# Attention with squared ReLU, then a feed-forward layer: one more batch in block form, and loads in permuted order

## The chip, the cores and the metric

The kernel runs on one core of one Trainium2 chip. The metric is the device time of one execution in microseconds. An execution is described by a profile with the times of every instruction on TensorE (PE, with its weight loads PEld), VectorE (DVE), ScalarE (ACT), GpSimd (POOL) and the queue of SyncE (SP), and of the DMA transfers.

## The reference, cut to what matters

There are 8 batches of 12 heads with 448 positions and 64 numbers a head. The attention has no softmax: scores are rectified, squared and divided by the length. Its output, 3584 rows of 768, goes through a layer to 2048 columns, an exact GELU, and a layer back to 768.

```python
scores = scale * np.matmul(q, k.transpose(0, 1, 3, 2))
attn = np.maximum(scores, 0.0) ** 2 / S
attn_out = np.matmul(attn, v)
x = attn_out.transpose(0, 2, 1, 3).reshape(B * S, H * D)
h = x @ w_in
g = 0.5 * h * (1.0 + erf(h * inv_sqrt2))
return g @ w_out
```

## The kernel before, in words

Inputs come as float32 and are cast to bf16 by the loading DMAs, which GpSimd issues. A batch is worked in three groups of four heads (g = 0 to 2), and each group in seven blocks of 64 key rows (i = 0 to 6).

**Attention.** One score step (`fn_qk`, L686) makes four 64x64 tiled matmuls of 448 columns into a PSUM pair. ScalarE (L698) or VectorE (L700) rectifies and scales it into a bf16 tile `a_sq`, and VectorE squares that in place (L707). After seven steps, `add_av` (L746) multiplies by the values, 28 matmuls, and two copies bring the result to `xT` (L400 and L402 are the lines of the copy helper).

**Feed-forward.** `add_f1` makes one tile of the first layer, 128 of the 2048 columns: six matmuls of 448 columns (L800) and a GELU on ScalarE (L810) into the ring `h_sb`, which holds two batches. The second layer goes over 14 groups of 256 rows (`add_group`, L1108); each group is a two-by-two block product done with seven products instead of eight, at the price of sums on VectorE (L1089, L1142). The first 256 rows are done plainly (L1203).

**Block form of the first layer.** For batches 5, 6 and 7 (`add_blocks`, L942) the first layer also takes seven products instead of eight, on halves of the inner dimension, of the columns and of the 448 rows, so that a matmul has 224 columns. It needs sums of weight quarters (`add_wsums`, L867), made once while batch 7's attention runs, sums of the input's quarters (L909), and adds of partial results (L976).

**Order of the work.** A planner written in Python runs when the program is built. It knows a duration for each operation, due times worked out over several passes, and how many buffers there are, and fixes each engine's order. The first part of the order is written out by hand (`ORDER`: a letter for the engine, a number for the operation). From batch 2 on, TensorE's order is a fixed list. Batches 0 and 1 do their attention beside the first layer of batch 0. Batches 2 to 7 each have six slots, and after each slot come as many feed-forward products as a share (`SHARES`) gives it:

```python
            x = [("QK", (b, g, i, None)) for i in range(NK)]
            mid = ("AV", done) if done else ("FFN", None)
            out.append(x[:2] + [mid] + x[2:4])
            out.append(x[4:])
```

So a group's value product stands among the first steps of the next group. The products that fill the slots are the rest of batch 1's first layer, the plain rows, groups 1 to 6, and the first layers of batches 2, 3 and 4. After the last value product come, with no attention beside them, the blocks of batches 5 to 7 woven with groups 7, 9 and 11, and the groups 8, 10, 12 and 13.

**Queries and keys.** A score step needs both transposed. Batches 0 and 1 are loaded contiguously and transposed by TensorE. Batch 2 is loaded contiguously too, and VectorE copies it in permuted order (`permute_k` L529, `permute_q` L540) into the pair `pq`, `pk`. From batch 3 on, `add_wide` loads queries and keys in that permuted order straight into the pair, 64 numbers to a run: six DMAs of keys (L467) and twelve of queries (L476) for a batch. The one pair serves all batches, so a load waits until the transposes of the batch before have read it (`war`). From the pair, SP issues seven transposing DMAs (`add_T_dma`, three for keys at L632, four for queries at L641) into `kT` and `qT`, which exist twice. They're allowed from a given slot of the batch before on.

**GpSimd's queue** is strictly in order. It holds the loads of batches 0, 1 and 2 and the first layer's weights, the first part of the second layer's weights `wout` (L372), a small copy `gate` that waits for the transposed queries of batch 2 (L653), the other two parts of `wout`, batch 3's keys, queries and values, and then for each batch a gate and the load of the batch after next.

Of the kernel before, what the change touches and what calls it, by code (L numbers as in the profile page):

```python
# [13 lines left out]
KC = 112  # L14
# [21 lines left out]
T_TWO = 0.72  # L36
# [8 lines left out]
DMA_FREE = 4.54  # L45
# [8 lines left out]
SHARES = (1.3, 1.0, 1.0, 1.0, 1.0, 1.0)  # L54
LAST = 256
PASSES = 5
NEAR = 0.5
# [4 lines left out]
WIDE = 2.0  # L62
# [13 lines left out]
G0 G1 G2 G3 G4 G5 A10 D13 G6 A16 P11 P14 G7 D12 A15 P17 G8 D18 P21 P39 D22 P33 P36 A34 D40  # L76
P19 D20 A37 P23 G9 P42 P48 D24 P54 A43 D35 A49 P51 D44 P25 D38 A52 D41 G117 A55 D53 P45 D50
A26 D47 A46 P57 D56 P69 P66 A58 D70 P27 G118 A67 P29 D59 P63 G119 A28 D71 P60 A64 G120 D68
P78 D61 A62 P75 A79 D65 P81 P31 D30 A76 D80 P96 G121 D32 A97 P72 D77 G122 A82 D98 P129 G123
D74 A73 P90 D130 P84 P108 A91 G124 D83 P131 A85 D109 P93 P141 D132 A94 D92 P102 D95 P105  # L80
P111 A103 D86 P143 D110 G125 A106 D104 P99 A112 D107 G126 A144 P87 D100 A101 D113 A142 P157
P114 D88 G127 A158 D89 P133 D115 A116 G128 P135 D159 A134 P160 P163 D136 P166 A164 P145 D167
A161 D165 P253 A146 D168 D162 P169 P172 G147 A254 P175 A173 D170 P245 G148 A176 D171 P255
A246 D177 G149 D174 P184 P187 A256 P196 A185 G150 D188 P137 P139 A138 P178 D197 G151 A140
D186 P193 P211 G152 D180 P247 A212 G153 D213 P249 A248 D179 A194 D198 G154 P263 A250 D195
D229 G155 P223 P220 A264 D189 P190 S235 A224 D221 P265 G156 A191 D225 P267 A266 D192 D222
P199 P217 A268 P214 D231 A218 P257 S236 D215 A200 D219 P259 A258 D216 D201 P181 P208 A260
P205 D230 A209 P261 D182 P251 D183 A262 D210 A206 D233 P202 A252 S237 D207 D232 P226 D234
A203 D204 S238 S239 P269
# [17 lines left out]
class Scheduler:  # L107
# [151 lines left out]

    def place(self, fixed):  # L260
# [14 lines left out]
        while rest or any(fixed.values()):  # L275
# [7 lines left out]
            for e, v in fixed.items():  # L283
                if v and not (e == "PE" and by.get("PE")):
                    tops.append(self.pick(v[:1]))
# [11 lines left out]
def kernel(  # L297
# [37 lines left out]
    def get_nat(b):  # L335
        if b not in nq:

            tq, tk = ("pq", "pk") if b == 1 else ("nq", "nk")
            nq[b] = natpool.tile([KC, H, NC * D], BF16, tag=tq, name="nq")
            nk[b] = natpool.tile([128, HP, NK * D], BF16, tag=tk, name="nk")  # L340
            vt[b] = vpool.tile([128, HP, NK * D], BF16, tag="v", name="v_sb")

# [34 lines left out]
    pqk = []  # L377

    def get_p():
        if not pqk:  # L380
            pqk.append(natpool.tile([KC, NC, DM], BF16, tag="pq", name="pq"))
            pqk.append(natpool.tile([128, G, NK * 128], BF16, tag="pk", name="pk"))
        return pqk
# [40 lines left out]
    def war(b):  # L424

        old = [o for (bb, *_), o in list(Pq.items()) + list(Pk.items()) if bb == b - 1]
        c = {1: -1, 2: 0}.get(b, b - 1)
        old += [o[0] for (bb, *_), o in list(Tq.items()) + list(Tk.items()) if bb == c]
        return old
# [19 lines left out]
    def add_v(b, g0, g1):  # L449
        def fn():  # L450
            get_nat(b)
            nc.gpsimd.dma_start(vt[b][:, 2 * g0 : 2 * g1], kv_view(v, b, g0, g1))  # L452

        old = [o for (bb, *_), o in AV.items() if bb == b - 3]
        o = dma(fn, (g1 - g0) * 4 * S * 256, old)
        for g in range(g0, g1):
            ld_v[b, g] = [o]

    def add_wide(b):


        def k_fn(e):
            def fn():
                to = get_p()[1].rearrange("p g (i e d) -> e p g i d", e=2, d=D)
                src = kv_view(k, b, 0, G).rearrange("p (g e) (i d) -> e p g i d", e=2, d=D)
                for g in range(G):
                    nc.gpsimd.dma_start(to[e][:, g], src[e][:, g])  # L467

            return fn

        def q_fn(e, j):
            def fn():
                to = get_p()[0].rearrange("p c (g j e d) -> j e g p c d", j=2, e=2, d=D)
                src = q[b].rearrange("(g e j) (p c) d -> j e g p c d", e=2, j=2, c=NC)
                for g in range(G):
                    nc.gpsimd.dma_start(to[j][e][g], src[j][e][g])  # L476

            return fn

        def v_fn():  # L480
            vt[b] = vpool.tile([128, HP, NK * D], BF16, tag="v", name="v_sb")
            nc.gpsimd.dma_start(vt[b], kv_view(v, b, 0, G))

        n = G * 4 * S * 256
        ks = [dma(k_fn(e), WIDE * n / 2, war(b), G) for e in range(2)]
        qs = [dma(q_fn(e, j), WIDE * n / 4, war(b), G) for e in range(2) for j in range(2)]
        old = [o for (bb, *_), o in AV.items() if bb == b - 3]
        o = dma(v_fn, n, old)
        ops = Both(ks), Both(qs)
        for g in range(G):  # L490
            ld_v[b, g] = [o]
            Pk[b, g] = ops[0]
            for c in range(NC):
                Pq[b, g, c] = ops[1]

    class Both:


        def __init__(self, ops):
            self.ops = ops  # L500

        @property
        def done(self):
            ends = [o.done for o in self.ops]
            return None if None in ends else max(ends)

    def add_load(b, g0=0, g1=G):
        if b > 2:
            return add_wide(b)
        add_k(b, g0, g1)  # L510
        add_q(b, g0, g1)
# [14 lines left out]

    def permute_k(copy, g, src):

        copy(  # L529
            get_p()[1][:, g].rearrange("p (i e d) -> p e i d", e=2, d=D),  # L530
            src.rearrange("p e (i d) -> p e i d", d=D),
        )

    def permute_q(copy, g, c0, c1, src):

        dst = get_p()[0][:, c0:c1, 256 * g : 256 * g + 256].rearrange(
            "p c (j e d) -> e p j c d", j=2, d=D
        )
        for e in range(2):
            copy(dst[e], src[:, 2 * e : 2 * e + 2].rearrange("p j (c d) -> p j c d", d=D))  # L540

    def add_pk(b, g0, g1, after=(), bias=0.0):
        for g in range(g0, g1):
            deps = ld_k[b, g] + list(after)
            deps += [Tk[max(b - 1, 1), x, i][0] for x in range(G) for i in range(NK)]
            Pk[b, g] = sch.add(
                (("DVE", 0.31, 0.43),),
                lambda e, g=g: permute_k(V.tensor_copy, g, nk[b][:, 2 * g : 2 * g + 2]), deps,
                bias=bias,
            )  # L550

    def add_pq(b, g0, g1, c0=0, c1=NC, after=(), bias=0.0):
        for g in range(g0, g1):
            deps = [ld_q[b, g, c] for c in range(c0, c1)] + list(after)
            deps += [Tq[max(b - 1, 1), g, c][0] for c in range(c0, c1)]
            if b == 2:
                deps += [Tq[1, x, c][0] for x in range(G) for c in range(NC)]
# [896 lines left out]
```

## Time and profile before

| What | Value |
|---|---|
| time, median of three runs | 371.25 us (370.54 to 372.1) |
| the profiled execution | 370.77 us |
| its span, first to last instruction | 368.9 us |
| TensorE busy | 358.9 us, 97% of the span |
| VectorE busy | 288.3 us, 78% |
| ScalarE busy | 200.8 us, 54% |
| GpSimd busy | 108.0 us, 29% |
| software DMA queue | 74,992 packets, 22.47 MB, 58.6% of 16 engines |
| hardware DMA queues (SP's) | 38,768 packets, 19.46 MB, 26.8% |
| TensorE's granted clock | 0.999 |

Busy shares are means over stages. From about 65 to 252 us the attention of batches 2 to 7 runs with its feed-forward products between; from 252 to 364 the closing products alone. Times of single matmuls in the profile overlap, as they're pipelined, so a group's length is read from where the next one starts. A wait is put down to the one that came last.

### The profile page before, as it was taken

Reading aid. Unit: us, or ns where it says so; the run is one execution under the profiler, and the core shown is the slowest. Engines: PE = TensorE matmul, PEld = TensorE weight load, DVE = VectorE, ACT = ScalarE, POOL = GpSimd, SP = SyncE. Lnnn points to the kernel's source line nnn. Section 1 sums busy time; section 2 is a strip of 40 time slices with the busy share of each in tenths; the row PEclk is TensorE's granted clock in tenths of the full one; section 3 lists DMA queues with packets and bytes.
Section 4 is the critical chain, followed back from the end, with each engine's and each line's share of the span. In section 5 each row is a group of like instructions: output and inputs, shape, how many; then the busy total and the mean of one; then the engine's idle time right before and its main releaser. Section 6 shows DMA issues by size and latency. Waiting matters only on the chain.

```text
span 368.9 us, 8544 instructions
## 1 busy us (share of the span) xinstructions
PE 358.9 (97%) x3557; PEld 222.1 (60%) x3557; DVE 288.3 (78%) x493; ACT 200.8 (54%) x308; POOL 108.0 (29%) x149
## 2 busy tenths in 40 slices
PE   8799999999999999999999999999999999999994
PEld 7566645455544455544455545457886897688663
DVE  2998991789868978987699888888998658665862
ACT  4988865664447845677755588853440353044200
POOL 8666401726087096097095000000000000000000
PEclk9999999999999999999999999999999999999999
DMA  9999999999999999999999960003002301310233
GB/s 174 196 200 204 202 189 134 173 171 131 244 135 167 160 85 172 209 163 154 146 93 133 205 117 2 3 0 87 2 0 88 85 2 29 109 36 2 85 85 88
DMA packets 114166, 42.98 MB, mean 116 GB/s; under 512 B 92816, under 2 KB 110672, under 8 KB 114128
## 3 DMA queue, kind: packets, MB, share of 16 engines
q0 software_dynamic: 74992, 22.47, 58.6%
q1 hardware_dynamic: 38768, 19.46, 26.8%
q8 instruction: 28, 0.46, 0.5%
q10 hardware_dynamic: 368, 0.51, 0.4%
q14 instruction: 10, 0.08, 0.1%
HBM read 45.61 MB, written 11.01 MB: 153 GB/s over the span
## 4 chain that ended last, share of the span: by engine, by line
PE 87%; DMA 4%; DVE 4%; ACT 2%; POOL 1%; issue 1%; DVEq 0%; POOLq 0%; ACTq 0%
PE pso L1108 32%; PE psh L800 24%; PE pb L942 13%; PE ps L686 8%; PE pav L746 6%; PE pso L1203 3%; DMA v_sb<-in_v_dram 2%; DVE a_sq L707 2%; DMA nk<-in_k_dram 2%; ACT a_sq L698 2%; POOL nk L434 0%; POOL v_sb L452 0%; POOL nq L349 0%; PE tp L580 0%; DVE a_sq L700 0%
## 5 line engine op out<-in xcount | busy, mean ns | idle before, releaser
L698 ACT ACTIVATE a_sq<-ps 128x896 bf16<-128x896 f32 (+1 forms) x136 | 117.4, 914 | 44.6 <-PE ps L686 44.5
L707 DVE TENSOR_TENSOR a_sq<-a_sq 128x896 bf16<-128x896 bf16 (+1 forms) x169 | 97.5, 617 | 7.5 <-ACT a_sq L698 7.2
L800 PE MATMUL psh<-xT,win_sb 128*128 128x448 bf16 (+1 forms) x516 | 96.6, 340 | 0.1
L800 PEld LDWEIGHTS <-win_sb 128*128 128x128 bf16 x516 | 47.8, 98 | 45.5 <-issue 10.2
L810 ACT ACTIVATE h_sb<-psh 128x448 bf16<-128x448 f32 x80 | 43.9, 549 | 24.1 <-PE psh L800 23.9
L1108 PEld LDWEIGHTS <-s_sb 128*128 128x128 bf16 x424 | 40.6, 98 | 27.0 <-issue 2.2
L700 DVE TENSOR_SCALAR a_sq<-ps 128x896 bf16<-128x896 f32 x33 | 35.9, 1090 | 18.3 <-PE ps L686 17.8
L686 PE MATMUL ps<-qT,kT 64*64 64x448 bf16 (+1 forms) x756 | 47.3, 336 | 2.2 <-ACT qT L402 0.6
L976 DVE TENSOR_TENSOR part<-pb,part 128x448 f32<-128x448 f32 x60 | 34.6, 619 | 18.4 <-PE pb L942 18.4
L476 POOL DMA_DIRECT2D pq<-in_q_dram x60 | 41.8, 704 | 10.1 <-DVE a_sq L707 6.4
L1108 PEld LDWEIGHTS <-h_sb 128*128 128x128 bf16 x312 | 29.9, 98 | 21.1 <-issue 2.5
L1108 PE MATMUL pso<-wout_sb,s_sb 128*128 128x384 bf16 (+2 forms) x216 | 38.1, 320 | 0.3 <-DVE osb L1142 0.3
L1108 PE MATMUL pso<-wout_sb,h_sb 128*128 128x384 bf16 x208 | 38.1, 326 | 0.0
L1108 PE MATMUL pso<-t_sb,s_sb 128*128 128x384 bf16 x208 | 38.1, 326 | 0.0
L746 PE MATMUL pav<-a_sq,v_sb 64*64 64x448 bf16 (+1 forms) x756 | 36.8, 330 | 0.7 <-ACT a_sq L698 0.4
L686 PEld LDWEIGHTS <-kT 64*64 64x64 bf16 x756 | 18.3, 105 | 24.2 <-issue 17.4
L985 ACT ACTIVATE h_sb<-part 128x448 bf16<-128x448 f32 x36 | 19.8, 578 | 19.9 <-DVE part L976 19.8
L467 POOL DMA_DIRECT2D pk<-in_k_dram x30 | 28.9, 966 | 1.5 <-issue 0.9
L746 PEld LDWEIGHTS <-v_sb 64*64 64x64 bf16 x756 | 21.1, 107 | 13.0 <-issue 2.3
L942 PEld LDWEIGHTS <-win_sb 128*128 128x128 bf16 x288 | 27.6, 98 | 2.2 <-issue 0.4
L1142 DVE TENSOR_TENSOR osb<-pso,p_sb 128x384 f32<-128x384 f32 x39 | 21.7, 556 | 8.2 <-PE pso L1108 5.7
L400 DVE CAST xT<-pav 128x448 bf16<-128x448 f32 (+1 forms) x43 | 23.7, 583 | 4.6 <-PE pav L746 3.9
(62 smaller groups left out, 292.0 us busy)
## 6 DMA issues: line engine op xcount, KB each, us to landing
pk<-in_k_dram POOLq DMA_DIRECT2D x30, 112.0 KB, 4.4
pq<-in_q_dram POOLq DMA_DIRECT2D x60, 56.0 KB, 5.0
v_sb<-in_v_dram POOLq DMA_DIRECT2D x5, 672.0 KB, 9.1
out_dram<-osb SPq DMA_DIRECT2D x8, 336.0 KB, 3.0
wout_sb<-in_moe_w_out_dram POOLq DMA_DIRECT2D x2, 1152.0 KB, 12.1
v_sb<-in_v_dram POOLq DMA_DIRECT2D x9, 224.0 KB, 8.8
out_dram<-osb SPq DMA_DIRECT2D x7, 288.0 KB, 3.4
out_dram<-osb SPq DMA_DIRECT2D x8, 240.0 KB, 3.1
```

Source lines behind the costliest of these rows:

```text
L467: nc.gpsimd.dma_start(to[e][:, g], src[e][:, g])
L476: nc.gpsimd.dma_start(to[j][e][g], src[j][e][g])
L686: nc.tensor.matmul(ps[64 * j : 64 * j + 64, e, x * w : x * w + w], kT[r, g, i * 128 + 64 * j : i * 128 + 64 * j + 64], qT[r, 2 * g + j, co ...
L698: A.activation(ar, ps, AF.Relu, scale=c_att)
L700: V.tensor_scalar(ar, ps, c_att, 0.0, op0=mybir.AluOpType.mult, op1=mybir.AluOpType.max,)
L707: V.tensor_mul(box["a2"][:, :, :used], ar, ar)
L746: nc.tensor.matmul(pav[0][o2 : o2 + 64, e, :w], vt[b][r, 2 * g + e, bass.ts(i, D)], box["a2"][r, e, o : o + w], start=(i == 0), stop=(i == ...
L800: nc.tensor.matmul(ph[:, x * n : x * n + n], win_sb[:, kd, bass.ts(m + x, 128)], xT[b][:, kd, c], start=(kd == 0), stop=(kd == KD - 1),)
L810: A.activation(h_ring()[:, m : m + nm, o + c.start : o + c.stop], box[0][:, :S].rearrange("p (x n) -> p x n", x=nm), AF.Gelu,)
L942: nc.tensor.matmul(bank[name][:, y, z * HS : z * HS + HS], w[:, k, bass.ts(mm, 128)], right()[:, k], start=first and k == 0 and z == 0, st ...
L976: V.tensor_add(get(to), ps(name), get(other))
L1108: nc.tensor.matmul(box[bank][:, n0:n1], left()[:, kf], right[:, kf, n0:n1], start=bool(need) and kf == 0, stop=kf == K2 - 1, skip_group_ch ...
```

## The change

Batch 4's first layer leaves the attention slots and is done as blocks behind them, woven with group 6, which leaves the slots too; both stand ahead of the blocks of batch 5. The first layer of batch 4 no longer comes before the weight sums. Batch 2's queries and keys are loaded in permuted order as well, and VectorE's copies for it go. Permuted data gets a second pair of buffers: odd batches use `pq` and `pk`, even ones `nq` and `nk`. So the load of a batch waits for the transposes of the batch before last, and batch 4's load stands right after batch 3's in GpSimd's queue; from then on each gate is followed by the values of one batch and the queries and keys of the next. The transposes may start from the first slot of the batch before (batch 3's as before). A slot now holds three score steps; the value product stands in the group's second slot. If TensorE's next score step or value product would have to wait in the plan, the planner may take the next feed-forward product in its place (`pick_pe`). The inputs of batch 4's blocks are summed in the buffer of `qT`, and those of the later batches take the buffers in turn. In `ORDER` the six copies are taken out and the later numbers are shifted by six; the sequence of the others stays.

```diff
-DMA_FREE = 4.54
+DMA_FREE = 3.05
-SHARES = (1.3, 1.0, 1.0, 1.0, 1.0, 1.0)
+SHARES = (1.3, 1.1, 1.0, 1.0, 1.0, 1.0)
+PULL = 0.15
+PULL_IN = 0.45
-NEAR = 0.5
+NEAR = 0.25
...
+    def pick_pe(self, v):
+        top = self.pick(v[:1])
+        wait = math.inf if top is None else top[1] - self.free["PE"]
+        if v[0].mode == "F" or wait <= (PULL if self.mode == "F" else PULL_IN):
+            return top
+        nxt = next((o for o in v if o.mode == "F"), None)
+        other = nxt and self.pick([nxt])
+        if other and other[1] - self.free["PE"] <= PULL and other[1] < self.free["PE"] + wait:
+            return other
+        return top
...
-    def get_p():
+    def get_p(b):
+        if b % 2 not in pqk:
+            tq, tk = ("pq", "pk") if b % 2 else ("nq", "nk")
...
     def war(b):
-        old = [o for (bb, *_), o in list(Pq.items()) + list(Pk.items()) if bb == b - 1]
-        c = {1: -1, 2: 0}.get(b, b - 1)
+        c = {1: -1, 2: 0, 3: 1}.get(b, b - 2)
...
+    def add_wide_k(b, g):
+        def fn():
+            to = get_p(b)[1].rearrange("p g (i e d) -> e g p i d", e=2, d=D)
+            src = kv_view(k, b, 0, G).rearrange("p (g e) (i d) -> e g p i d", e=2, d=D)
+            for e in range(2):
+                nc.gpsimd.dma_start(to[e][g], src[e][g])
+        Pk[b, g] = dma(fn, 4 * S * 256, war(b), 2)
+    def add_wide_q(b, g):
+        def fn():
+            to = get_p(b)[0].rearrange("p c (g j e d) -> j e g p c d", j=2, e=2, d=D)
+            src = q[b].rearrange("(g e j) (p c) d -> j e g p c d", e=2, j=2, c=NC)
+            for e in range(2):
+                for j in range(2):
+                    nc.gpsimd.dma_start(to[j][e][g], src[j][e][g])
...
     def add_load(b, g0=0, g1=G):
-        if b > 2:
-            return add_wide(b)
-        add_k(b, g0, g1)
-        add_q(b, g0, g1)
+        if b < 2:
+            add_k(b, g0, g1)
+            add_q(b, g0, g1)
+        else:
+            for g in range(g0, g1):
+                add_wide_k(b, g)
+                add_wide_q(b, g)
         add_v(b, g0, g1)
...
-                    tag = {B - 3: "qT", B - 2: "kT", B - 1: "qT"}[b]
+                    tag = {B - 4: "qT", B - 3: "kT", B - 2: "qT", B - 1: "kT"}[b]
...
-            out.append(x[:2] + [mid] + x[2:4])
-            out.append(x[4:])
+            out.append(x[:3])
+            out.append(x[3:5] + [mid] + x[5:])
...
-    for g in range(G):
-        add_pk(2, g, g + 1, bias=T_TWO)
-        add_pq(2, g, g + 1, bias=T_TWO)
     add_T_dma(2, [[]] * 7)
     add_gate(2)
...
-    add_load(3)
+    add_wide(3)
+    add_v(3, 0, G)
+    add_wide(4)
-    F1B = {2: 1, 3: 2, 4: 3, 5: 4}
-    GROUPS = {2: (1,), 3: (2, 3), 4: (4, 5), 5: (6,)}
+    F1B = {2: 1, 3: 2, 4: 3}
+    GROUPS = {2: (1,), 3: (2, 3), 4: (4, 5)}
...
-            n = {2: 2, 3: 2}.get(b, 1)
+            n = {2: 2}.get(b, 0)
             add_T_dma(b + 1, [at(b, n + (y >= 4)) for y in range(7)])
             if b + 2 < B:
                 add_gate(b + 1)
-                add_load(b + 2)
+                add_v(b + 2, 0, G)
+                if b + 3 < B:
+                    add_wide(b + 3)
...
-    end = woven(add_blocks(B - 3), add_group(7))
+    end = woven(add_blocks(B - 4), add_group(6))
+    end += woven(add_blocks(B - 3), add_group(7))
     end += add_group(8)
```

## Prediction

> **What bounds the kernel now.** I read three stretches first: the end of the first attention batches, the attention batches 2 to 7 (65 to 252 us), and the closing stretch. The columns are the stretch, its length, then busy us of TensorE, of its weight loads, of VectorE, ScalarE and GpSimd, then clock, DMA share and GB/s.
>
> ```profile
> 30.00:55.00 25.00, 24.92 (x294) 14.36 (x287) 22.91 (x41) 19.68 (x30) 8.45 (x12) 1.00 1.29 197
> 65.00:252.00 187.00, 186.16 (x1745) 95.61 (x1744) 159.57 (x261) 119.32 (x169) 76.29 (x100) 1.00 1.16 131
> 252.00:364.00 112.00, 112.00 (x907) 87.05 (x904) 81.50 (x143) 34.03 (x66) 0.00 (x0) 1.00 0.18 52
> ```
>
> TensorE idles 0.84 us in 187 and not at all in the last 112. So TensorE's work is the bound, and only fewer or cheaper matmuls can shorten it. The Trainium skill, page "Perfetto Trace Analysis", section "Identifying the Most-Contended Engine", warns that matmul busy time overstates, since matmuls are pipelined; I therefore price by the chain of waits, where pieces follow each other without overlap (start, us, what):
>
> ```profile
> 163.70 3.51 PE psh L800 x18
> 167.91 3.51 PE psh L800 x18
> ...
> 250.66 1.45 PE pav L746 x28
> 252.10 2.41 PE pb L942 x24
> 254.51 1.30 PE pso L1108 x8
> 255.81 3.45 PE pb L942 x36
> 259.26 1.30 PE pso L1108 x8
> 260.56 4.60 PE pb L942 x48
> ```
>
> The closing stretch is one unbroken chain of TensorE. Between the two L800 pieces lie 0.70 us, three score steps of 0.19 plus 0.13 for changing over. Last I read GpSimd's order of time, as its queue carries all loads:
>
> ```profile
> 43.51 0.76 POOL L372 DMA_DIRECT2D wout_sb<-in_moe_w_out_dram  x1 [0.37 <-DMA nq<-in_q_dram]
> 63.48 0.19 POOL L653 COPY gate<-qT 128x4 bf16<-128x4 bf16 x1 [19.21 <-DMA qT<-pq]
> 63.71 1.65 POOL L372 DMA_DIRECT2D wout_sb<-in_moe_w_out_dram  x2
> 65.69 5.78 POOL L467 DMA_DIRECT2D pk<-in_k_dram  x6 [0.33 <-PE ps L686]
> ...
> 101.71 0.19 POOL L653 COPY gate<-qT 128x4 bf16<-128x4 bf16 x1 [12.42 <-DMA qT<-pq]
> ```
>
> The gate copy runs when a batch's transposed queries are there: 63.48 for batch 2, whose scores begin at 65.02, and 101.71 for batch 3, whose scores begin at 107.19. These are the slacks that the change spends: about 1.5 and 5.5 us.
>
> **What the skill says.** Page "TensorE: Matmul & The Clock Gate", section "Back-to-back issue gap": N/2.4 + 2.5 ns, so 189 ns for 448 columns and 95.8 for 224. The trace agrees: (3.51 - 2.38)/6 = 188 ns between L800 pieces of 18 and 12, and (4.60 - 2.30)/24 = 95.8 ns at L942. Page "DMA: Bandwidth & Descriptors", section "Specifications": transfers want 512 bytes for line rate. Batch 2 would now come in 256-byte runs of float32. The trace agrees that short runs are slower: early contiguous loads move about 200 GB/s, batch 7's permuted load, with the queues nearly its own, 82 to 112; but there GpSimd's issues (0.966 us for 112 KB of keys, 0.70 for 56 KB of queries) already set that rate, and landings stayed at 3.2 to 4.2 us.
>
> **Part 1, batch 4 in block form.** Removed: 16 tiles of 6 matmuls of 448 columns, 96 x 0.188 = 18.1 us. Added: 7 products x 4 tiles x 6 matmuls of 224 columns, 168 x 0.0958 = 16.1 us. TensorE saves **2.0 us**, all on the path. Added on VectorE are 20 sums of 0.619 (L976) and four operand sums of 0.50, on ScalarE 4 copies; the gelus are as many columns as before. They fall into the closing stretch, where VectorE is 73% and ScalarE 30% busy and where three batches of the same form run without a gap: nothing. Their buffer comes free with batch 6's scores, a whole batch ahead. If that cover failed, a wait would show between pb pieces, up to about 1 us.
>
> **Part 2, what leaves the attention stretch.** Batch 4's first layer (18.1 us) and group 6 (seven products of 1.30, 9.1 us) move behind it. The stretch shrinks from 187 to about 160 us. The moved TensorE work costs the same later, so itself nothing. But VectorE and ScalarE must serve the same six batches in less time. They have 159.6 + 119.3 = 278.9 us there now, 75% of two engines. Sixteen gelus (8.8) and group 6's sums and passes (4 x 0.685 + 7 x 0.556 = 6.6) go, which leaves 263.5 us, 83% of 2 x 160. If the rectifiers stayed where they are, VectorE alone would have 153 of 160; some of its 23 (1.09 each) have to go to ScalarE (0.917). The cover is shown to be possible: 30 to 55 us ran at (22.91 + 19.68)/50 = 85% and TensorE missed 0.08 us. It's thinner at the end, as eight weight sums of 0.95 and four operand sums of 0.50 must fit beside batch 7. Bounds: -0.8 (every present gap closed) to +4 (2.5% of 160); I take **+0.5**.
>
> **Part 3, batch 2 loaded permuted.** Nine permuting copies leave VectorE (3 x 0.385 + 6 x 0.286 = 2.9 us, at 42 to 54); TensorE has no gap there, so nothing gained. Nine issues of about 0.71 become 21: 6 x 0.966 + 12 x 0.70 + 3 x 0.70 = 16.3 us on GpSimd. They start at 33.1 as now. The last query's issue ends at about 48.7 instead of 42.2. Queued behind are wout's first part, the gate of batch 2, two more wout parts and batch 3's loads; behind the landings, SP's three kT and four qT transposes. Before, the last nq landed at 52.0 and the copies ended at 53.7; then qT's transposes took from 54.96 to 61.90 and the gate saw them at 63.48. After: 48.7 plus a landing of 3.2 (quiet) to 10.5 (the slowest of the nq loads) gives 52 to 59; I take 6.5, so 55.2, plus 6.9 of transposes plus 1.6 is 63.7. Scores can still start at 65.0. Bounds: 0 to +3; I take **+0.3**.
>
> **Part 4, two buffer pairs.** Batch 3's load still stands behind the gate of batch 2 and both wout parts, so its queries land near 95 and its gate falls near 101.7 as now. But the plan weighs the slots' products at 8 x 1.14 + 4 x 2.6 + 6 x 9.1 + 3 x 18.24 = 128.8 us, and at 101.5 without group 6 and one first layer; batch 2's share of them falls from 128.8 x 1.3/6.3 = 26.6 to 101.5 x 1.3/6.4 = 20.6 us, so batch 3's scores are wanted about 6.3 us earlier (6.0 by 1.05, the ratio of real to planned time), at 100.9. Here the slack becomes -0.8, and batch 4's load, now issued straight after, runs beside the qT transposes. The new rule that lets TensorE take a ready feed-forward product when its next score product has to wait can fill this, at about 0.25 us for each pair of changeovers. Bounds 0 to +3; I take **+0.4**. From batch 4 on, loads run a batch ahead; GpSimd needs 14.2 + 0.9 us for one of about 26.6, so that's covered. Transposes come earlier in SP's queue; the stores that stand behind them there wait for nothing new, as the data they transpose has landed by then, and their three row buffers come free as before.
>
> **Part 5, value products in the second slot.** The same matmuls in as many changeovers, and the squares get a longer lead; TensorE waited 0.4 us once for a square. Bounds -0.4 to 0; I take 0.
>
> **The sum.** -2.0 + 0.5 + 0.3 + 0.4 = -0.8 us. Against the profiled execution (370.77 us, of which 368.9 are the span and 1.9 lie around it) that is 370.0. That execution is 0.5 below the median of 371.25, inside the runs shown (370.54 to 372.1), so a median could come to 370.4; I keep **370.0**, as ready products may fill part of the waits that I added.
>
> **The rivals.** *The whole saving arrives* (chance 0.30): every handover hides and one or two of today's gaps close: -2.0 to -2.8, 368.2 to 369.2. For it: TensorE at 99.6% with 85% on the helpers at 30 to 55 us. Against: two slacks go from 1.5 and 5.5 us to about nothing. *The helpers become the bound* (0.15): in the last two batches weight sums, group sums and squares fill VectorE; 2 to 4 us of waits, 371 to 373. For it: VectorE was busy 27 of 30 us at 125 to 155 and 185 to 215 with fewer attention steps in them. *The loads of batches 2 and 3 come late* (0.18), the one that ends slower: the place is the qT transposes on SP. It decides when the last of batch 2's queries lands after 56.5 us (65.0 - 1.6 - 6.9). If short runs beside 200 GB/s of weights land in 14.6 us, as wout's first part did, it is 63.3, the scores start near 71.8 and TensorE loses 6.8 less what products it can take early, net 4 to 5; the gate, wout and batch 3 shift with it. Then 373 to 376. *The change doesn't act*, the block sums costing what they save (0.02): 371. My forecast, part of the saving eaten by short waits, has 0.35: 369 to 371.2.
>
> **How the numbers follow.** About 0.5% (1.86 us) is what a measurement of this kernel can tell from no change: faster is below 369.4, slower above 373.1. Faster: the whole saving 0.30 and a fifth of the forecast, 0.37. Slower: late loads 0.17 and half of the helpers' case, 0.25. The rest, 0.38, is no change. The range runs from 368.2 to 374.6, leaving out the tails of late loads and a better closing of gaps.
>
> **What would show it.** L942 should have 672 matmuls instead of 504, L800 96 fewer (420), the closing chain 25 us more, the attention stretch about 160. Batch 2's scores should start at 65 to 66, batch 3's near 101 to 103, with no psh or ps piece waiting over 1 us. VectorE and ScalarE together near 83% of the stretch. The forecast is wrong if TensorE's busy time falls by less than 1.5 us, or if its gaps between 55 and the start of the closing stretch exceed 4 us.

## The result, and the profile after

The changed kernel takes 385.47 us (median of four runs, 384.23 to 385.67) where the kernel before, run beside it, takes 371.68 (370.54 to 372.13): a ratio of 1.037, interval 1.0335 to 1.0403. It is slower by 13.8 us, outside the range forecast. The profiled execution took 385.6, of which 383.8 are the span; before they were 370.77 and 368.9.

The page of after first: the span, TensorE's row, its granted clock over 40 slices, and the issues of permuted keys and queries with KB each and median us to landing (from the issue until the data is there).

```profile
span 383.8 us, 8737 instructions
...
PE 361.2 (94%) x3629; PEld 229.2 (60%) x3629; DVE 291.9 (76%) x500; ACT 208.8 (54%) x320; POOL 118.6 (31%) x161
...
PEclk9999999999899969999999999999999999999999
...
pk<-in_k_dram POOLq DMA_DIRECT2D x36, 112.0 KB, 11.0
pq<-in_q_dram POOLq DMA_DIRECT2D x72, 56.0 KB, 6.6
```

TensorE is busy 2.3 us longer than before (358.9), though it was given 2 us less to do, and its clock dips in two slices, the deeper near 140 us. Keys take 11.0 us to land; the same row of before says 4.4 (queries 5.0). Next the stretches of after, with the columns of the first fence of the prediction: batch 2 with the wait for batch 3, then to batch 4's first scores, then the rest of the attention, then the closing stretch.

```profile
67.39:109.77 42.38, 38.01 (x320) 19.27 (x319) 30.59 (x47) 21.32 (x31) 27.82 (x36) 0.96 1.56 174
109.77:136.22 26.45, 21.54 (x210) 9.73 (x211) 19.03 (x31) 19.70 (x28) 14.94 (x20) 0.96 1.66 166
136.22:241.35 105.13, 104.43 (x1063) 53.17 (x1063) 94.79 (x162) 73.14 (x97) 35.36 (x47) 0.98 1.12 114
241.35:383.00 141.65, 137.73 (x1132) 108.60 (x1128) 102.70 (x183) 46.45 (x90) 0.00 (x0) 1.00 0.18 51
```

TensorE idles 4.37 and 4.91 us in the first two stretches (length less its busy time) and 0.70 in the 105 us after them. The whole account, in us:

| Piece | Before | Worked out for the change | After | Difference |
|---|---|---|---|---|
| batch 2's first scores | 65.02 | 65.02 | 67.39 | +2.37 |
| from there to the closing stretch | 187.02 | 187.02 - 27.2 = 159.8 | 173.96 | +14.1 |
| from there to the end | 116.9 | 116.9 + 25.2 = 142.1 | 142.45 | +0.4 |

The differences add up to 16.9 us; less the 2.0 that the block form saves, that is the 14.9 by which the span grew. So the loss lies in the attention of batches 2 to 4. TensorE's order of time shows where (start, us, what; in brackets the idle time ahead and its releaser):

```profile
67.39 0.76 PE L643 MATMUL ps<-qT,kT 64*64 64x448 bf16 x12 [2.00 <-DMA qT<-pq]
...
95.18 0.38 PE L643 MATMUL ps<-qT,kT 64*64 64x448 bf16 x4 [2.09 <-DVE a_sq L657]
95.50 4.45 PE L1160 MATMUL pso<-wout_sb,h_sb 128*128 128x384 bf16 x16
...
109.77 0.76 PE L643 MATMUL ps<-qT,kT 64*64 64x448 bf16 x12 [1.77 <-DMA qT<-pq]
...
136.22 1.33 PE L643 MATMUL ps<-qT,kT 64*64 64x448 bf16 x12 [4.68 <-DMA qT<-pq]
137.49 5.15 PE L757 MATMUL psh<-xT,win_sb 128*128 128x448 bf16 x18
```

Three waits of 2.00, 1.77 and 4.68 us are for transposed queries, one of 2.09 is for VectorE; with three short ones of 0.2 to 0.5 they make 11.5. Behind two of them the same matmuls take longer: 16 of the plain rows 4.45 us (2.77 where none has waited), 18 of the first layer 5.15 (3.51 in the prediction's chain, 3.58 as this view counts), a score piece 1.33 instead of 0.76. That is 1.68 + 1.57 + 0.57 = 3.8 us at a lower clock: the record of the granted clock has a mean of 0.61 in 95.5 to 99.9 us and 0.65 in 136.2 to 142.6. Of the 14.1 us the idle time is 10.0, less the 0.84 of before, and the clock 3.8; about 1 us is left unexplained.

GpSimd's order of time shows the loads that belong to it (gates, wout, then batch 4's keys and queries):

```profile
67.41 0.18 POOL L610 COPY gate<-qT 128x4 bf16<-128x4 bf16 x1 [12.78 <-DMA qT<-pq]
67.64 1.64 POOL L389 DMA_DIRECT2D wout_sb<-in_moe_w_out_dram  x2
...
92.33 1.92 POOL L481 DMA_DIRECT2D pk<-in_k_dram  x2
...
107.26 0.70 POOL L491 DMA_DIRECT2D pq<-in_q_dram  x1 [2.46 <-DMA pk<-in_k_dram]
...
115.00 0.23 POOL L610 COPY gate<-qT 128x4 bf16<-128x4 bf16 x1
```

Batch 2's gate falls at 67.41 instead of 63.48. Batch 4's load is issued from 92.33 to 115.00: 22.7 us, where the issues alone take some 14, since an issue waits for the landing of an earlier DMA ("<-DMA pk"). The waits fit the DMA eight places before: the issue at 99.44 waits for the values, which stand eight places ahead of it, that at 111.42 for the load's first query. So from 115 on the gate tells of GpSimd and not of the transposes. Within that time SP issues batch 3's transposes, and later batch 4's beside batch 5's load. The landing times in 120 to 129 us of after:

```profile
pk<-in_k_dram POOLq DMA_DIRECT2D x3, 112.0 KB, 14.4
pq<-in_q_dram POOLq DMA_DIRECT2D x3, 56.0 KB, 12.8
qT<-pq SPq DMA_TRANSPOSE x4, 9.8
```

The same four transposes in 121 to 129 us of before, beside the end of the values' load but no load of queries or keys:

```profile
qT<-pq SPq DMA_TRANSPOSE x4, 3.1
```

From the first issue to TensorE's (or the gate's) start they took 120.63 to 136.22 = 15.6 us in after and 122.19 to 128.93 = 6.7 in before. Batch 4's own load had come earlier than before (the first transpose is issued 1.6 us earlier); its transposes ended 7.3 us later. Batch 3's went the same way: issued from 96.15, done at 109.7 (13.6 us), against 94.90 to 101.7 (6.8); here SP also issued two stores between the transposes, 1.2 us, which in before stand behind them.

The closing chain answers to the second fence of the prediction:

```profile
241.41 2.41 PE pb L899 x24
243.82 1.30 PE pso L1065 x8
...
256.15 3.45 PE pb L899 x36
...
275.45 4.60 PE pb L899 x48
```

Pieces of 24, 36 and 48 block matmuls take 2.41, 3.45 and 4.60 us, as before: the block form was priced rightly.

### The profile page after: what moved, and what is told of

Read it like the earlier page. It is cut to its first block, busy times and chain, and to the rows that moved or that the text cites. A ratio compares the mean times of both kernels' runs of the same rounds, so it can differ in the third digit from the quotient of the medians.

```text
span 383.8 us, 8737 instructions
## 1 busy us (share of the span) xinstructions
PE 361.2 (94%) x3629; PEld 229.2 (60%) x3629; DVE 291.9 (76%) x500; ACT 208.8 (54%) x320; POOL 118.6 (31%) x161
## 4 chain that ended last, share of the span: by engine, by line
PE 59%; DMA 22%; DVE 7%; POOL 4%; issue 3%; SPq 2%; ACT 2%; DVEq 0%; POOLq 0%; ACTq 0%
PE pso L1065 24%; PE pb L899 15%; PE psh L757 11%; DMA pk<-in_k_dram 8%; PE ps L643 5%; DMA wout_sb<-in_moe_w_out_dram 4%; PE pav L703 3%; DMA qT<-pq 3%; DMA kT<-pk 3%; SPq L598 2%; DMA v_sb<-in_v_dram 2%; POOL pk L481 2%; DMA pq<-in_q_dram 2%; DMA nk<-in_k_dram 2%; DVE part L933 1%
## 5 line engine op out<-in xcount | busy, mean ns | idle before, releaser
L655 ACT ACTIVATE a_sq<-ps 128x896 bf16<-128x896 f32 (+1 forms) x139 | 119.6, 914 | 42.6 <-PE ps L643 42.5
L757 PE MATMUL psh<-xT,win_sb 128*128 128x448 bf16 (+1 forms) x420 | 79.5, 342 | 0.3 <-DVE osb L1099 0.2
L491 POOL DMA_DIRECT2D pq<-in_q_dram x72 | 50.7, 707 | 46.5 <-DMA pk<-in_k_dram 27.9
L933 DVE TENSOR_TENSOR part<-pb,part 128x448 f32<-128x448 f32 x80 | 46.0, 620 | 23.1 <-PE pb L899 23.1
L643 PE MATMUL ps<-qT,kT 64*64 64x448 bf16 (+1 forms) x756 | 48.6, 340 | 13.2 <-DMA qT<-pq 8.5
L1065 PEld LDWEIGHTS <-s_sb 128*128 128x128 bf16 x424 | 40.6, 98 | 26.6 <-issue 2.7
L657 DVE TENSOR_SCALAR a_sq<-ps 128x896 bf16<-128x896 f32 x30 | 32.6, 1090 | 16.3 <-PE ps L643 16.0
L767 ACT ACTIVATE h_sb<-psh 128x448 bf16<-128x448 f32 x64 | 34.9, 549 | 17.5 <-PE psh L757 17.5
L942 ACT ACTIVATE h_sb<-part 128x448 bf16<-128x448 f32 x48 | 26.8, 579 | 28.2 <-DVE part L933 27.9
L899 PEld LDWEIGHTS <-win_sb 128*128 128x128 bf16 x384 | 36.8, 98 | 2.8 <-issue 0.4
L481 POOL DMA_DIRECT2D pk<-in_k_dram x36 | 34.7, 968 | 3.3 <-issue 1.1
L899 PEld LDWEIGHTS <-ws 128*128 128x128 bf16 x288 | 27.6, 98 | 0.5 <-DVE part L933 0.5
```

Source lines behind the costliest of these rows:

```text
L481: nc.gpsimd.dma_start(to[e][g], src[e][g])
L643: nc.tensor.matmul(ps[64 * j : 64 * j + 64, e, x * w : x * w + w], kT[r, g, i * 128 + 64 * j : i * 128 + 64 * j + 64], qT[r, 2 * g + j, co ...
L655: A.activation(ar, ps, AF.Relu, scale=c_att)
L657: V.tensor_scalar(ar, ps, c_att, 0.0, op0=mybir.AluOpType.mult, op1=mybir.AluOpType.max,)
L757: nc.tensor.matmul(ph[:, x * n : x * n + n], win_sb[:, kd, bass.ts(m + x, 128)], xT[b][:, kd, c], start=(kd == 0), stop=(kd == KD - 1),)
L767: A.activation(h_ring()[:, m : m + nm, o + c.start : o + c.stop], box[0][:, :S].rearrange("p (x n) -> p x n", x=nm), AF.Gelu,)
```

## The experiments

Two theories were set against each other. The theory of the loads (L) says that queries and keys reach TensorE late, since a batch of attention is now shorter and loads and transposes share the DMA engines. The theory of the helpers (H in the expectations) says that VectorE and ScalarE can't serve six batches of attention in 160 us. A third (P) puts all harm on the permuted load of batch 2 and the early load of batch 4. All times are medians, beside runs of the kernel before (370.84 to 371.05 for these runs, 371.68 beside the changed kernel). So a difference between two changed kernels holds to within about 1 us. Line numbers differ a little from kernel to kernel.

### Which part of the change

**e1_block_only**: the kernel before, with only batch 4's block form and group 6 moved.

```diff
-    F1B = {2: 1, 3: 2, 4: 3, 5: 4}
-    GROUPS = {2: (1,), 3: (2, 3), 4: (4, 5), 5: (6,)}
+    F1B = {2: 1, 3: 2, 4: 3}
+    GROUPS = {2: (1,), 3: (2, 3), 4: (4, 5)}
...
-    end = woven(add_blocks(B - 3), add_group(7))
+    end = woven(add_blocks(B - 4), add_group(6))
+    end += woven(add_blocks(B - 3), add_group(7))
```

> The kernel before, with only batch 4's first layer in block form and group 6 moved behind the slots; loads, buffers and slots as before. Theory L (the loads are the new bound: the slots hold 27 us less work, and the transposed queries come too late for it): with one buffer pair a batch's gate-to-gate cycle was 26.2 to 28.3 us before, and a batch would now want 26.6 us, after a slack at batch 3 that shrinks from 5.5 to about -1; so TensorE waits 1 us at batch 3 and 0.5 to 1.5 us at each batch after it, 4 to 6 us in all, and the time is 372 to 376. Theory P (the permuted load of batch 2 and the early load of batch 4 are the harm, the block form is harmless): 368.5 to 370, no wait for transposed queries over 0.5 us. Theory H (VectorE and ScalarE can't keep up in the shorter stretch): 372 to 375, but with the waits on the rectified scores, not on qT.

Measured: 388.77 us, ratio 1.050 (1.0442 to 1.0563). TensorE waits 6.07 us for batch 4's queries (at 129.15), 2.84 for batch 6's, 2.26 for a rectified score on VectorE and some short ones. Every theory had expected less, 376 us at most. Batch 4's gate, 129.16, is where it was before (128.93): with one pair the load chain kept its pace, and TensorE arrived earlier.

**e3_plain4**: the changed kernel with batch 4 plain and group 6 back in the slots (the edit of e1 the other way).

> The changed kernel with batch 4's first layer and group 6 put back into the slots in plain form; batch 2 permuted, two pairs and the new slots stay. Theory L: the slots hold 27 us more, so batches 3 and 4 want their queries 6 to 8 us later, and the waits there vanish; what stays is the start of batch 2's scores (2.4 us late) and part of the wait of VectorE for wout: 373 to 376. Theory P (the loads themselves cost it whatever the slots hold): 380 or more. If the block form were all of the harm, this would return to 371.

Measured: 380.37 us, 1.025 (1.0225 to 1.0269). The rest of the change costs 9.5 us with no block form in it. TensorE waits 1.60 us for batch 2's queries, 0.84 at batch 3, 1.54 for VectorE, and 3.42 at 160.94 for a sum on VectorE, which itself waited 4.50 us for a row buffer still being stored; the stores had been issued behind transposes on SP. The waits at batches 3 and 4 went almost wholly, as the theory of the loads had it, but its 373 to 376 was too low: the number is the one that P had named (380 or more). The two parts don't add: the block form alone costs 17.9, the rest alone 9.5, both 13.8 to 14.6. Put under the block form, the rest even saves 3.3 us (388.77 to 385.47), but that is less than either costs.

**e4_b2nat**: the changed kernel with batch 2 contiguous and permuted by VectorE, as before; the pairs change places.

```diff
-            tq, tk = ("pq", "pk") if b % 2 else ("nq", "nk")
+            tq, tk = ("nq", "nk") if b % 2 else ("pq", "pk")
...
-        if b < 2:
+        if b < 3:
             add_k(b, g0, g1)
             add_q(b, g0, g1)
...
+    for g in range(G):
+        add_pk(2, g, g + 1, bias=T_TWO)
+        add_pq(2, g, g + 1, bias=T_TWO)
     add_T_dma(2, [[]] * 7)
```

> The changed kernel with batch 2 loaded contiguously and permuted by VectorE as before (the two pairs change places, so that batch 2 goes into pq and pk); the early loads of batches 4 to 7 stay. Theory P, batch 2 as the root: scores of batch 2 start at 65.0 instead of 67.4, all behind its gate moves up by 4 us, the waits at batches 3 and 4 go and the time is 369 to 372. Theory L: the start gains 2.4 us and batch 3 loses its wait of 1.8, but the load of batch 4 still runs beside batch 3's transposes and batch 5's beside batch 4's, so 2 to 5 us of waits stay: 376 to 381.

Measured: 381.37 us, 1.029 (1.0246 to 1.0338), 4.1 below the changed kernel. TensorE's order of time in this run:

```profile
109.68 1.33 PE L689 MATMUL ps<-qT,kT 64*64 64x448 bf16 x12 [7.33 <-DMA qT<-pq]
110.94 2.74 PE L1111 MATMUL pso<-t_sb,h_sb 128*128 128x384 bf16 x8
```

Batch 3's queries come at 109.7 as in the changed kernel, and now TensorE waits for them 7.33 us; eight matmuls then take 2.74 us instead of 1.46. So the permuted load of batch 2 is some 2 or 3 in 10 of the loss (4.1 of 13.8, or 3.3 when each kernel is taken against its own runs of before), and a batch that is early only waits longer at the next.

### Loads or helpers

Four kernels leave out DMAs of queries and keys; all other instructions stay, the transposes too, and work on the data that lies in the buffers. e5 and e9 skip batches 4 to 7, in the changed kernel and in e4; e6 and e7 skip 3 to 7, in e1 and in the kernel before.

```diff
     def add_wide_k(b, g):
         def fn():
+            if b > 3:
+                return
...
     def add_wide_q(b, g):
         def fn():
+            if b > 3:
+                return
```

> The changed kernel with the DMAs of queries and keys of batches 4 to 7 left out (those batches work on the data of batches 2 and 3 that lie in the two pairs); all transposes, values, products and the order of the other engines stay. Theory L: with no permuted load beside them the transposes of batches 3 and 4 land some 4 us after their issue and TensorE's waits of 1.8 and 4.7 us and the half clock behind them go; batch 2's late start (2.4 us) and the wait for VectorE near 93 us stay: 373 to 376. Theory H (VectorE and ScalarE are what's short): the waits only change their name, 380 to 385.

> The kernel before with batch 4 in block form and group 6 moved, as in the run of the block form alone, and with the queries and keys of batches 3 to 7 not loaded (they work on batch 2's). Theory L: nothing is left that could be late, and the block form earns its 2 us: 368.5 to 370 against the next run's 370.5 to 371.5. Theory H: 1 to 4 us of waits on rectified scores or squares stay, 371 to 374.

> The kernel before with the queries and keys of batches 3 to 7 not loaded, nothing else changed: the counterpart of the run before. All theories: TensorE hardly waited for loads in the kernel before, so 370 to 371.5.

> The changed kernel with batch 2 contiguous and copied by VectorE, and with the queries and keys of batches 4 to 7 not loaded (they work on those of batches 2 and 3). Theory L (all of the harm is that loads bring the transposed queries, and wout behind batch 2's gate, too late): both repairs together close the account, 369 to 370.5, with no wait over 1 us from batch 2 on. Theory H (part of it is that VectorE and ScalarE can't follow, as 6 us of waits on them stayed in the block form alone without loads): 372 to 375.

Measured: e5 374.65 us (1.011, 1.0073 to 1.0141), e6 380.03 (1.0235, 1.0198 to 1.0272), e7 372.20 (1.003, 1.0017 to 1.0038), e9 369.86 (0.997, 0.9957 to 0.998).

The loads of batches 4 to 7 cost the changed kernel 385.47 - 374.65 = 10.8 us, or 10.2 when each is taken against its own runs of before. They cost the kernel before nothing: e7 is even 1.2 us slower, with a wait of 0.91 us for wout at 81.16 that before doesn't have. The numbers of e5 and e9 lie in the ranges of the theory of the loads; e7's is 0.7 above its range, e6's is above both of its own. In e5 the transposes of batches 3 and 4 land in 3.2 us, TensorE waits 4.2 us in all instead of 11.5, and no piece runs slow: 7.3 + 3.8 = 11.1, near the 10.8. What e5 still waits for is batch 2: its scores start at 66.92, after a wait of 1.21, and VectorE holds TensorE up for 2.57 at 94.9. With batch 2 contiguous as well, e9 goes to 369.86. Its attention stretch:

```profile
65.43:225.59 160.16, 159.47 (x1594) 80.74 (x1593) 145.60 (x241) 113.56 (x156) 19.09 (x27) 1.00 0.74 114
```

Here are the 160 us that the prediction worked out: TensorE idles 0.69 us with the two helpers at (145.60 + 113.56)/320.3 = 81%. The helpers can do it, and the block form then pays, in a kernel that leaves loads out: 1.1 us below the kernel before, 2.3 below e7. Two buffer pairs, the new slots and `pick_pe` are in e9 too, so none of them costs much by itself. So the whole way from 385.47 is 10.8 for the loads and 4.8 for batch 2.

e6 says something else of the old plan. Its waits on TensorE are (releaser, us in total, times, longest):

```profile
PE ps L688 <- DVE a_sq L702: 4.3, 2, 2.3
PE ps L688 <- ACT a_sq L700: 2.0, 4, 0.8
PE ps L688 <- DMA qT<-pq: 1.7, 1, 1.7
```

With the old slots and planner 6.3 us go to the helpers even with no such loads at all (0.7 of them ahead of batch 2), and the kernel is 7.8 us above e7. H holds for the block form alone, and not for the changed kernel, whose slots and rule `pick_pe` go with it; which of these, or of the planner's new constants, helps was not separated.

### Loads one at a time

**e2_paced**: in the changed kernel a batch's load is issued behind the gate of the batch before, so no load runs beside the transposes that are wanted next.

```diff
     add_v(3, 0, G)
-    add_wide(4)
...
                 add_gate(b + 1)
+                add_wide(b + 2)
                 add_v(b + 2, 0, G)
-                if b + 3 < B:
-                    add_wide(b + 3)
```

> The changed kernel with each batch's queries and keys issued behind the gate of the batch before and ahead of its values, as in the kernel before; both buffer pairs, batch 2 permuted and the rest stay. Theory L in the form 'the early load of the batch after next delays the transposes that are wanted first': qT lands about 4 us after its issue instead of 8 to 10, the waits of 1.8 and 4.7 us at batches 3 and 4 shrink to under 2 together; but a load cycle of some 27 us a batch bounds the later batches, 0.5 to 1 us each: 376 to 381. Rival (batch 2's late start is the root, everything else follows it): no gain, 384 to 387. Theory H: unchanged, 384 to 387.

Measured: 388.29 us, 1.047 (1.0427 to 1.0522), above every range that was named; the landing came as the theory of the loads had it, the gain did not. In 121 to 133 us of this run batch 4's transposes land so:

```profile
qT<-pq SPq DMA_TRANSPOSE x4, 3.0
```

The gates, from GpSimd's order of time:

```profile
104.24 0.19 POOL L610 COPY gate<-qT 128x4 bf16<-128x4 bf16 x1 [12.18 <-DMA qT<-pq]
...
132.75 0.19 POOL L610 COPY gate<-qT 128x4 bf16<-128x4 bf16 x1 [11.84 <-DMA qT<-pq]
...
161.43 0.19 POOL L610 COPY gate<-qT 128x4 bf16<-128x4 bf16 x1 [11.05 <-DMA qT<-pq]
```

This separates the two costs. Alone, the transposes land in 3.0 us: what stretched them was the load beside them. But load and transposes, one after the other, now take 28.5 us for a batch (104.24 to 132.75), and TensorE wants one in 159.8/6 = 26.6. It waits for queries again, 4.98, 1.86 and 2.00, and 2.06 for a copy on VectorE. Before, with a stretch of 187 us, it wanted one in 31.2.

### More work ahead of batch 4

If TensorE wants the queries too early, products can be moved there. `SHARES` gives batch 3's slots more of them, and `LEADS` puts ten instead of four ahead of batch 3's first step. e8 does this to e4; e10 takes 1.9 and 0.8 in place of 1.5 and 0.9; e11 gives the changed kernel the shares of e10, and e12 gives them to e1.

```diff
-LEADS = {3: 4}
-SHARES = (1.3, 1.1, 1.0, 1.0, 1.0, 1.0)
+LEADS = {3: 10}
+SHARES = (1.3, 1.5, 0.9, 0.9, 0.9, 0.9)
```

> The changed kernel with batch 2 contiguous as in the earlier run, and the slots' products drawn forward: ten products ahead of batch 3's scores instead of four, batch 3's share 1.5 instead of 1.1, later ones 0.9. All loads stay as they are. Theory L: batch 3's scores are wanted 6 to 7 us later, when its transposes are done, so the wait of 7.3 us and its half clock (2.7 us) go; later batches have 23 us each, and loads that take 21 to 25 us a batch: 370 to 374. Theory H: the batches with less beside them starve on VectorE and ScalarE, 376 to 381.

> As the run with the slots' products drawn forward (batch 2 contiguous, ten leading products), with batch 3's share at 1.9 and later ones at 0.8, and all loads in place. Theory L: batch 4's scores are wanted 5 us later, when its queries are there; the wait of 5.2 us and its half clock (2.4 us) go: 369.5 to 372, level with the kernel before. Rival (the wait only moves on to batch 5, whose slots now hold less): 374 to 378.

> The changed kernel as it is, batch 2 permuted by its loads, with only ten leading products and the shares 1.3, 1.9 and four times 0.8. Theory L: the waits at batches 3 and 4 shrink, the late start of batch 2 (2.4 us) and the late wout behind its gate stay: 374 to 378, 4 to 5 us over the same with batch 2 contiguous. If the permuted load of batch 2 were harmless: within 1 us of it.

> The block form of batch 4 alone on the kernel before (one pair of buffers, loads behind the gates), with ten leading products and the shares 1.3, 1.9 and four times 0.8. Theory L: with one pair a batch's load, transposes and gate take 27 us and the later batches would want theirs every 23; waits of 3 to 4 us a batch from batch 5 on, 380 to 390. If one pair were enough: 370 to 373.

Measured: e8 378.18 us (1.020, 1.0161 to 1.0231), e10 377.02 (1.017, 1.0148 to 1.0194), e11 384.42 (1.036, 1.0308 to 1.0411), e12 383.81 (1.034, 1.0309 to 1.0363).

In e8 batch 3's wait is gone and one of 5.21 for batch 4's queries stands at 133.16; so the number falls into the range of H, but not for H's reason. In e10 that is gone too, and the longest wait of TensorE is another:

```profile
158.66 1.46 PE L1111 MATMUL pso<-t_sb,h_sb 128*128 128x384 bf16 x8 [2.88 <-DVE osb L1145]
```

It's the wait of e3: the sum waited 6.00 us for a row buffer whose store was issued behind four transposes that took SP 7.43 us. Another 2.32 us stand at 162.45 ahead of the next batch's scores, with no releaser in the record. So one wait moves down the line to the next place with little slack, as the rival had it (374 to 378). e10 is the best that does all the work, 6 us above the kernel before. e11 missed its expectation by 6.4 us: batch 2's permuted load is worth 7.4 us here, against 4.1 and 4.8 in the other pairs. Part of this shows in its trace: TensorE waits 3.21 us at 186.89 for a copy of batch 5's values into `xT` on VectorE, which takes the buffer `nk` and waited 4.38 us for batch 6's keys, the last to use it. The change itself brought this in, as even batches' keys now lie in `nk`; the 2.06 us of e2 are the same copy. Beside it stand 2.37 us for VectorE at 94.60, which e10 doesn't have, and more time at a lower clock behind these waits (16 plain-row matmuls 4.30 us for 2.77); the exact split is open. In e12, with one pair, the waits moved to batches 5 and 6 (1.33 and 5.23), and its number lies in the range that was named (380 to 390).

### Keys ahead, queries behind

Last I tried to load only the keys of the batch after next ahead of a gate, and its queries behind it: e13 in e8, e14 in e4, e15 in the changed kernel.

```diff
-    add_wide(4)
+    for g in range(G):
+        add_wide_k(4, g)
...
                 add_gate(b + 1)
+                for g in range(G):
+                    add_wide_q(b + 2, g)
                 add_v(b + 2, 0, G)
                 if b + 3 < B:
-                    add_wide(b + 3)
+                    for g in range(G):
+                        add_wide_k(b + 3, g)
```

> Batch 2 contiguous, ten leading products and shares 1.3, 1.5, 0.9 as in the first run with products drawn forward, and each batch's keys issued ahead of the gate of the batch before, its queries and values behind it. If traffic beside the query transposes is what delays them: qT of batches 3 and 4 lands 3 to 5 us after its issue instead of 8 to 10, batch 4's is there at 126 and wanted at 128, no wait over 1 us: 369 to 371.5. If the lateness of the loads is: queries behind the gate arrive later still, waits of 3 to 6 us at batches 4 to 6: 376 to 382.

> The same without the products drawn forward (four leading products, shares 1.3, 1.1, 1.0). Traffic: batch 3's queries are there some 4 us earlier than the 109.6 of the run with batch 2 contiguous, so its wait of 7.3 us falls to 2 to 4: 373 to 377. Lateness: no gain, 381 or more.

> The changed kernel with only the order of the loads altered in that way (batch 2 permuted by its loads, shares as in the change). Traffic: the waits at batches 3 and 4 shrink from 6.4 to 2 to 4 us, the late start of batch 2 and the late wout stay: 378 to 382. Lateness: 385 or more.

Measured: e13 383.16 us (1.031, 1.0281 to 1.0343), e14 386.95 (1.042, 1.0381 to 1.0464), e15 390.73 (1.052, 1.0482 to 1.055): 5.0, 5.6 and 5.3 us worse than the kernels they were made from. In e13 the keys' DMAs still lie beside the transposes of batches 3 and 4, which land in 7.6 and 8.4 us, and the queries now start only behind the gate; its gates come every 26.4 to 26.7 us, a pace set by the chain. So e13 tests the traffic theory only in part. In e14 what that theory said of batch 3 came true: its queries are there at 105.61 instead of 109.68, and the wait falls from 7.33 to 4.35. But 4.81 at batch 4 and 2.34 at batch 6 outweigh it, so that the numbers of e14 and e15 are those of lateness, and e13's is 1.2 above them. No version that does all the work beat the kernel before.

## Why the prediction was wrong, point by point

**Part 1 was right.** The block pieces have the durations that it used, L899 (the old L942) has 672 matmuls and the first layer's row 420, and the closing stretch came within 0.4 us of 142.1.

**Part 2 was right for the changed kernel, and right only with its slots.** The stretch of 160 us with helpers at 83% (263.5 of 320 us are in fact 82%) exists, as e9 with 81% and 0.69 us of idle time shows. With the old slots it doesn't (e6). The rival "the helpers become the bound" isn't what happened.

**Part 3 was mis-sized.** Batch 2's scores started 2.4 us late, inside the bounds of 0 to +3, but 0.3 was taken. The 16.3 us for 21 issues had no pauses in them. On the chip they ran from 33.81 to 53.84, 20.0 us, as issues waited for landings; in before, too, the nine issues took from 33.28 to 43.14, 9.9 us, and not 9 x 0.71 = 6.4. So the last query's issue ended at 53.12 and not at 48.7:

```profile
50.29 2.83 POOL L491 DMA_DIRECT2D pq<-in_q_dram  x4
```

The transposes began at 58.29 (55.2 in the sum) and took SP 7.64 us (6.9). And the term ended at the scores, while the delay went on: batch 2's gate came 3.9 us later, with it the other two parts of wout, and with these the weight sums on VectorE. Its order of time in the changed kernel:

```profile
63.39 0.96 DVE L1003 TENSOR_TENSOR t_sb<-wout_sb 128x1536 bf16<-128x1536 bf16 x1 [7.65 <-DMA wout_sb<-in_moe_w_out_dram]
...
76.78 0.96 DVE L1003 TENSOR_TENSOR t_sb<-wout_sb 128x1536 bf16<-128x1536 bf16 x1 [2.47 <-DMA wout_sb<-in_moe_w_out_dram]
```

VectorE stands 11.4 us in three such waits, 2.7 in before; the longest, 7.65, is for wout's first part, queued behind batch 2's load. The sums then bunch with the squares, and TensorE loses 2.09 us at 95.18 (2.57 in e5); in e4, e9 and e10, with batch 2 contiguous, it waits there 0.2 at most. e4 and e9 put the part's full price at 3.3 to 4.8 us (7.4 between e11 and e10). I had named wout as queued behind the load, and not followed who waits for wout.

**Part 4 is the step that failed.** It took +0.4 us for the transposed queries of batches 3 and 4; their waits and the slow matmuls behind them came to 1.77 + 4.68 + 2.1 = 8.6. The sentences "its gate falls near 101.7 as now" and "GpSimd needs 14.2 + 0.9 us for one of about 26.6, so that's covered" looked at issue times alone. I had seen that batch 4's load "runs beside the qT transposes", and bounded the term by 3 us, without asking how long transposes take beside a load. The trace of before has the answer, for keys: in 128 to 150 us, beside batch 5's load, three transposes land in

```profile
kT<-pk SPq DMA_TRANSPOSE x3, 6.6
```

and in e5, from 125.39 and beside no more than the end of a load of values, in 3.1. In the changed kernel the query transposes of batches 3 and 4 took 7.8 and 9.8 us to land instead of 3.6 and 3.1. The sizes: in e5, where SP issues the same sequence without these loads, batch 4's queries are there 7.0 us after the first issue and batch 3's 8.1, against 15.6 and 13.6. The differences, 8.6 and 5.5, are more than the waits of 4.68 and 1.77. e5 and e2 show the cause, in that the stretch of the query transposes goes when the loads go. Nor did the covered 14.2 us hold: batch 4's load took 22.7 to issue.

Part 4 hoped that the new rule would fill such waits. It couldn't: `pick_pe` acts in the plan, and the plan prices every transposing DMA at 3.0 us from start to data, whatever runs beside it (`("SP", 1.2, 3.0)` in `add_T_dma`); a wait that the plan doesn't see is not filled.

That "the stores that stand behind them there wait for nothing new" was wrong as well, though the changed kernel's trace shows only 0.2 us of it: in e3 and e10 it is the longest wait, 3.42 and 2.88 us.

**A term was missing: the clock.** 3.8 us went to matmuls at about half rate behind waits. The Trainium skill, page "TensorE: Matmul & The Clock Gate", section "What's actually happening", has the clock fall to half after an idle window of some 3.4 us. The trace agrees with the half rate (1.33 us for 0.76) behind 4.68 us of idle; behind 2.09 it fell too (4.45 for 2.77), and behind 2.57 at the same place in e5 it didn't (16 matmuls 2.77), so the length alone doesn't decide.

**The rival that came nearest** is "the loads of batches 2 and 3 come late". It had the direction and the place, SP's transposes, but put the loss at batch 2 and gave 373 to 376; the larger part arose at batches 3 and 4 and from another cause, the loads beside the transposes. The mark set for a failure, gaps of over 4 us between 55 us and the closing stretch, was passed with 11.5; so was the other, as TensorE's busy time rose by 2.3 us instead of falling.

**Open.** How the 10.8 us split between the stretched transposes and the load's slower issue, which e5 removes together; whether some other order of loads lets the block form keep its 1 to 2 us; the rest of e11; about 1 us of the stretch. The change also took out a factor of 2 (`WIDE`) in the planner's price of a permuted load; no run puts it back. It isn't the whole cause, as e1 and e12 keep it and are no faster.

## What to carry to other kernels

When work is taken out of a loop whose bound is the compute engine, the loop's period shrinks for everything that feeds it: compare the new period (here 26.6 us) with the whole chain of load, transpose and handover for one round, not with the issue time of a queue. Running the next round's load beside this round's last step shortens the chain only if that step isn't slowed by it, so look for its duration in a stretch where both run. And price a wait on TensorE as its length plus what the matmuls behind it lose in clock, then ask where the next slack is used up: here a wait that was moved away from batch 3 came back at batch 4 (e8), and moved from there at batch 5 (e10).

## What the runs showed of the hardware

The transposing DMAs' time to landing depends on what runs beside them: 3.0 to 3.6 us with little else (e5, e2, before), 7.6 to 9.8 us beside permuted loads (after, e13), and SP's issue of four of them grew from 5.2 to 7.9 us. Short runs are not needed for it: in before, batch 2's three key transposes stand beside contiguous loads (30 to 64 us):

```profile
kT<-pk SPq DMA_TRANSPOSE x3, 9.8
```

In e5, too, three key transposes from 103.47, beside stores and a whole load of values, took 8.8. The loads suffer as well (keys 4.4 to 11.0 us in the pages' medians). And TensorE's half rate followed waits of 2.09 (in after), 4.68 and 7.33 us (e4), which cost 1.7 to 2.7 us more each time, but not one of 2.57 (e5).
